# A new order for all engines, six dummy blocks, and a split of the last half step in an attention kernel

## The chip, the cores and the metric

The kernel runs on one core of a Trainium2 chip. The metric is the device time of one launch in microseconds. A profiled execution gives, beside it, the span from the first to the last recorded instruction of the core. The engines are TensorE (PE in the profile, with its weight loads as PEld), VectorE (DVE), ScalarE (ACT), GpSimd (POOL) and SyncE (SP); DMAs are issued by SyncE and, at the very start, by ScalarE.

## The reference

Two layers of attention follow each other, in 32-bit floats. Cut to what matters:

```python
# layer 1: q, k, v are (8, 8, 576, 64); row i sees keys i-63 .. i
scores = where((rel >= 0) & (rel < 64), q @ k^T / 8, -1e9)
attn = exp(scores - max); attn /= sum + 1e-9
x = (attn @ v), heads side by side            # (8, 576, 512)
# layer 2: 4 experts, each row takes the 2 with the largest logits
logits = x @ w_gate; w = softmax over the 2 chosen logits (sum + 1e-9)
for each expert e:
    a = causal softmax of (x wq[e]) (x wk[e])^T / 8      # 576 x 576
    out += (w of e where chosen) * (a @ (x wv[e]) @ wo[e])
```

## The kernel before, in words

**Stage 1 (layer 1).** The 64 heads are taken as 32 pairs, two heads side by side on the 128 partitions; a pair has nine blocks of 64 queries. Eight such blocks make a unit, and there are 36 units u. For each unit `s1_qk` computes the scores of a query block against its own and the previous key block (block letter `s`, two PSUM banks), then the softmax: copies on ScalarE, masked copies with `own`, maximum and sum on VectorE, the subtraction and the division on GpSimd (tile `sm`, small tile `st`), the exponential on ScalarE. `s1_t` transposes the weights on TensorE (`t`, tile `t`, then `ft` and `pt`) and masks them, on VectorE and GpSimd for the first nine units (`u < JOIN`, a product with `tri`), on GpSimd alone for the others. `s1_av` multiplies with v (`a`, tile `o`) and splits the result x into a high and a low part (`xh` on ScalarE, `xl` on VectorE), so that three fast products give one of full precision (`three`).

**Stage 2 (layer 2).** It goes in half steps (b, pr): batch b = 0 to 7, experts 2pr and 2pr+1. `K`, `k`, `Q`, `q` are the projections in two halves each (`kps`, `qps`, tiles `kt`, `qt`), `V` and `W` the values of a block of rows of all experts, and with them the logits, from which `s2_gate` makes the gate `g` in small steps, most on VectorE and two products on GpSimd (lines 680 and 681 of the kernel before). `1`, `2`, `3`, `4` and `0` are the scores in a burst. `s2_soft` finds row minima on VectorE (custom instruction, tile `p`) and takes the exponential on ScalarE. `s2_w` makes the factors r and multiplies p with r and g on GpSimd, nine products in a half step. VectorE transposes 32 by 32 pieces into `st`, and 16 DMAs from SyncE put these in place as `pt`; only in the last half step (`TAIL = 1`) TensorE transposes (`T`, `U`). `A` and `B` multiply with the values, `s2_o` multiplies with wo (`O`, for the last batch `o` and `O`), copies the tile and stores it.

**What sets the order.** No engine call is issued where it is written. The class `Plan` (lines 83 to 347) records all calls, links them by the tiles they use and writes each engine's queue by a simulation with costs of its own (`length`, `SWITCH`, `HOP`, `OVERLAP`). TensorE's queue is fixed by the string `ORDER`, one letter for one block, and within a letter in the order of the calls. The other engines take, among the calls that are ready in that simulation, the one with the earliest due time: what TensorE needs first, shifted by a number of its own from the table `EARLY`. All blocks of TensorE share eight PSUM banks. All instructions are therefore issued from one line, L345, and the profile is read by tiles.

## Time and profile before

| | |
|---|---|
| median of 3 runs | 425.3 us (424.87 to 425.34) |
| profiled execution, device time | 425.67 us |
| its span | 423.9 us |
| mean granted clock of TensorE | 0.984 |
| TensorE busy | 400.3 us (94%) in 5109 products |
| VectorE busy | 320.6 us (76%) |
| ScalarE busy | 266.9 us (63%) |
| GpSimd busy | 269.1 us (63%) |

The device time is the span and 1.8 us around it. Busy time counts from the start of an instruction to its end; a product of two 32-bit tiles of stage 1 shows as two records, since it takes two passes. The granted clock is the share of full speed that the chip allowed TensorE: 1.00 is 2.4 GHz, 0.50 is 1.2 GHz. In a timeline, a row with `x16` is a run of sixteen like instructions, and the bracket says how long the engine had been idle before the first of them and which engine or DMA ended that.

### The profile page before, as it was taken

To read this page: it belongs to the slowest core of one execution; us is meant where nothing else is said; L and a number is where in the kernel's file an instruction comes from. 1 tells how busy PE (TensorE), PEld (TensorE's weight loads), DVE (VectorE), ACT (ScalarE), POOL (GpSimd) and SP (SyncE) were. 2 spreads that over 40 slices of the span, in tenths; PEclk is the share of its full clock that TensorE was granted. 3 is DMA by queue.
4 is the path that set the end of the run, shared out by engine and by line. 5 is a ranking of instruction groups with operands and counts; after the bars stand their busy time and mean duration, and the time that the engine had idled before them with its cause. 6 is when DMAs were issued, how large, how long until landed. Compare 5 with 4: busy or idle time off the path is not lost.

```text
span 423.9 us, 13636 instructions
## 1 busy us (share of the span) xinstructions
PE 400.3 (94%) x5109; PEld 360.6 (85%) x5109; DVE 320.6 (76%) x1033; ACT 266.9 (63%) x845; POOL 269.1 (63%) x437
## 2 busy tenths in 40 slices
PE   4589999999999999999999999999999999998795
PEld 3478989898989989889989998988988989897584
DVE  4789998979895877779796897769788668568322
ACT  2547667676868575676668477585668755563742
POOL 4668776787697747595787749864797551505040
PEclk9669999999999999999999999999999999999999
DMA  7966672267796860676866566666775524552703
GB/s 241 331 242 207 199 234 94 65 172 236 194 318 185 251 193 3 160 199 191 278 225 161 176 167 239 169 172 173 200 202 164 123 57 114 141 140 57 184 26 125
DMA packets 34129, 74.27 MB, mean 175 GB/s; under 512 B 6416, under 2 KB 10512, under 8 KB 34064
## 3 DMA queue, kind: packets, MB, share of 16 engines
q1 hardware_dynamic: 33488, 72.88, 58.5%
q8 instruction: 41, 0.67, 0.6%
q10 hardware_dynamic: 576, 0.52, 0.4%
q14 instruction: 24, 0.20, 0.2%
HBM read 39.85 MB, written 9.44 MB: 116 GB/s over the span
## 4 chain that ended last, share of the span: by engine, by line
PE 65%; DVE 15%; SPq 5%; POOL 5%; ACT 3%; DMA 3%; issue 3%; ACTq 0%; DVEq 0%; POOLq 0%
PE o L345 14%; PE s L345 12%; PE kps L345 9%; PE qps L345 9%; PE ops L345 9%; PE v2ps L345 9%; DVE st L345 6%; SPq L345 5%; PE t L345 4%; POOL p L345 3%; DMA k<-in_kT_dram 2%; DVE p L345 2%; DVE pt L345 1%; ACT p L345 1%; DVE sm L345 1%
## 5 line engine op out<-in xcount | busy, mean ns | idle before, releaser
L345 POOL TENSOR_SCALAR p<-p,r,g 128x320 f32<-128x320 f32 (+4 forms) x144 | 88.9, 634 | 42.9 <-DVE r L345 31.4
L345 POOL TENSOR_SCALAR_AFFINE_SELECT pt<-ft 64x512 f32<-64x512 f32 x126 | 84.4, 670 | 28.1 <-ACT ft L345 20.3
L345 POOL TENSOR_TENSOR sm<-sm,st 128x512 f32<-128x512 f32 x72 | 76.0, 1057 | 37.6 <-DVE st L345 26.8
L345 ACT ACTIVATE p<-p,r 128x320 f32<-128x320 f32 (+4 forms) x144 | 83.0, 578 | 17.3 <-DVE r L345 16.8
L345 PE MATMUL o<-pt,v 128*64 128x64 f32 (+2 forms) x1820 | 84.8, 252 | 6.6 <-DMA pt<-st 2.7
L345 PEld LDWEIGHTS o<-pt,v 128*64 128x64 f32 x1820 | 73.2, 140 | 19.2 <-issue 5.7
L345 DVE STREAM_TRANSPOSE st<-p 128x64 f32<-128x64 f32 (+2 forms) x135 | 68.4, 523 | 15.3 <-POOL p L345 10.2
L345 DVE CUSTOM_DVE_ANT_0 p<-s,causal 128x320 f32<-128x320 f32 (+2 forms) x128 | 56.2, 485 | 8.5 <-PE s L345 8.2
L345 DVE TENSOR_REDUCE st<-sm 128x8 f32<-128x512 f32 x72 | 48.3, 675 | 5.5 <-ACT sm L345 4.7
L345 PE MATMUL s<-kt,qt 64*128 64x256 f32 (+2 forms) x480 | 43.5, 319 | 2.2 <-ACT qt L345 0.9
L345 PE MATMUL s<-k,q 64*64 64x128 f32 (+1 forms) x1116 | 38.5, 278 | 6.7 <-DMA k<-in_kT_dram 6.7
L345 PEld LDWEIGHTS s<-kt,qt 64*128 64x128 f32 x480 | 35.9, 185 | 8.2 <-DVE qt L345 1.4
L345 PEld LDWEIGHTS s<-k,q 64*64 64x64 f32 x1116 | 31.9, 139 | 11.1 <-DMA q<-in_qT_dram 4.4
L345 PE MATMUL qps<-xh,wqhi 128*128 128x256 f32 (+1 forms) x128 | 39.0, 304 | 0.0
L345 PE MATMUL kps<-xh,wkhi 128*128 128x256 f32 (+1 forms) x128 | 38.8, 303 | 0.1
L345 PE MATMUL qps<-xh,wqlo 128*128 128x256 f32 (+1 forms) x128 | 37.6, 294 | 0.0
L345 PE MATMUL kps<-xh,wklo 128*128 128x256 f32 (+1 forms) x128 | 37.6, 294 | 0.0
L345 PE MATMUL qps<-xl,wqhi 128*128 128x256 f32 (+1 forms) x128 | 37.6, 294 | 0.0
L345 PE MATMUL kps<-xl,wkhi 128*128 128x256 f32 (+1 forms) x128 | 37.6, 294 | 0.0
L345 PE MATMUL v2ps<-wvhi,xh 128*128 128x260 f32 x128 | 37.2, 290 | 0.0
L345 DVE COPY_PREDICATED sm<-own,s 128x256 f32<-128x256 uint8 x72 | 29.0, 436 | 10.1 <-ACT sm L345 9.4
L345 PE MATMUL v2ps<-wvhi,xl 128*128 128x260 f32 x128 | 36.3, 283 | 0.0
(109 smaller groups left out, 893.9 us busy)
## 6 DMA issues: line engine op xcount, KB each, us to landing
v<-in_vW_dram SPq DMA_DIRECT2D x28, 576.0 KB, 4.8
pt<-st SPq DMA_DIRECT2D x120, 116.0 KB, 2.3
pt<-st SPq DMA_DIRECT2D x120, 80.0 KB, 2.1
out_dram<-out SPq DMA_DIRECT2D x32, 256.0 KB, 2.3
q<-in_qT_dram SPq DMA_DIRECT2D x28, 288.0 KB, 4.5
k<-in_kT_dram SPq DMA_DIRECT2D x28, 288.0 KB, 4.5
out_dram<-out SPq DMA_DIRECT2D x8, 128.0 KB, 2.4
v<-in_vW_dram SPq DMA_DIRECT2D x3, 320.0 KB, 7.0
```

The costliest lines, as they stand in the source:

```text
L345: call(*args, **kw)
```

## The change

1. `ORDER` and `EARLY` are new throughout, and so are the costs in `Plan` (changes of shape on TensorE, 100 ns after a GpSimd operation where 40 stood, lengths of GpSimd's operations, DMAs). Every engine's queue has another order. With few exceptions, named below, the instructions are the same ones.
2. Six dummy blocks `z` are added near the start of TensorE's queue: each multiplies the identity matrix with itself twice into a PSUM bank that nobody reads.
3. In the last half step (7, 1) the factors and products are taken in four smaller parts before the last one, as scores come, and the five products with even x run on VectorE, the four others on GpSimd as before.
4. The last output tile (batch 7, j = 4) is computed in two banks of 256 columns. One is copied by VectorE, the other by ScalarE, and the second of its two stores is issued by ScalarE.
5. `own` has a second half, made by one more cast on VectorE. The function `s1_d` and the sizes with `SHORT` are not used (`TPE` is 99, `SHORT` is 0). The gate's two products on GpSimd are the same as before.

```diff
@@ order and constants
 ORDER = (
-    "ssststaatsQQtassKVtVaatssqVtkastaKt1saa2V34Wts0kVqKtVQas1324tqVV0kstKQaAaBsat132"
...
-    "VBAk132V0VVK4kABOq3Q1OO240BATOToTTUoUoUoUoUABOOOOO"
+    "szsszztzstzatzsatQssaatVKQKtassatkqVtass12tVVs3taaq4s0WtKVQqkVs1aV3240tkKVktssaA"
...
+    "0VOKVOVBAQVqk12304KABOOQkq12340OOBATToTTUoUoUoUoUABOOOOO"
 EARLY = {
-    0: -22550, 2: -1250, 3: -50, 4: 2550, 5: -7250, 6: -1450, 7: -1850, 8: 22350, 9: 51250, 10: 3450,
+    0: -900, 1: 18550, 2: -6300, 3: -2950, 4: 700, 5: 34950, 6: 3750, 7: 7200, 8: 57850, 9: 27550,
...
+SHORT = 0
+WARM = 6
+TPE = 99
@@ class Plan
-    SWITCH = {(64, 64, F32): 90, (128, 64, F32): 140, (128, 128, F32): 155, (64, 128, F32R): 180, (128, 128, F32R): 200}
-    HOP = 40
+    SWITCH = {(64, 64, F32): 130, (128, 64, F32): 170, (128, 128, F32): 130, (64, 128, F32R): 220, (128, 128, F32R): 240}
+    HOP = {e: 100 if e == "G" else 40 for e in "PVAGS"}
...
+        op["lap"] = -50 if engine == "G" and outs[0].shape[0] <= 64 else self.OVERLAP[engine]
...
-            return {"tensor_tensor": 60 + 1.97 * n, "affine_select": 190 + 0.94 * n,
-                    "memset": 100 + 0.7 * n}.get(name, (265 if outs[0].shape[0] > 64 else 190) + 0.83 * n)
+            if name == "tensor_scalar" and len(ins) > 1:
+                return 342 + 0.85 * n
+            return {"tensor_tensor": 190 + 1.67 * n, "tensor_mul": 190 + 1.67 * n, "affine_select": 170 + 0.96 * n,
+                    "memset": 100 + 0.7 * n}.get(name, 190 + 0.84 * n)
@@ dummies
+    def warm(k):
+        ps = psum.tile([128, 512], F32, tag="s", bufs=8, name=f"warm_{k}")
+        with nc.block("z"):
+            for i in range(2):
+                nc.tensor.matmul(ps[:, 0:128], lhsT=ident, rhs=ident, start=True, stop=True)
...
+    todo += [(-9.0, warm, (k,)) for k in range(WARM)]
@@ s2_soft and s2_w
         if k == 1:
             least(banks[0][:, 448:512], P2[0][:, 0:64], m_f[:, 1], r2[:, 0, 0:1])
             exp(P2[0][:, 0:64], 0)
-            s2_w(b, pr, 0)
+            if not last:
+                s2_w(b, pr, 0)
...
+        if last and k < 2:
+            for x0 in ((1, 3), (0, 5))[k]:
+                s2_w(b, pr, 0, (x0, x0 + 2 if x0 else 1))
...
-            nc.gpsimd.tensor_scalar(p, p, r2[:, 2, x:x + 1], G2[b % 2][:, pr, x:x + 1], op0=OP.mult, op1=OP.mult)
+            engine = nc.vector if last and x % 2 == 0 else nc.gpsimd
+            engine.tensor_scalar(p, p, r2[:, 2, x:x + 1], G2[b % 2][:, pr, x:x + 1], op0=OP.mult, op1=OP.mult)
@@ s2_o
+        end = b == NB - 1 and j == 4
+        banks = [psum.tile([128, DM // (1 + end)], F32, tag="s", bufs=8, name=f"ops_{b}_{j}_{i}") for i in range(1 + end)]
...
-        if b < NB - 1 or j % 2:
+        if end:
+            nc.vector.tensor_copy(t[:, 0:256], banks[0])
+            nc.scalar.activation(t[:, 256:512], banks[1], AF.Copy)
+        elif b < NB - 1 or j % 2:
...
-                nc.sync.dma_start(out[b - 1 + i, 512:576], t[64 * i:64 * i + 64])
+                (nc.scalar if i and end else nc.sync).dma_start(out[b - 1 + i, 512:576], t[64 * i:64 * i + 64])
```

Three places in the queues, as the two kernels issue them.

ScalarE's queue at its very start, before. `k_74` holds the keys of the first pair, `k_76` of the second, `k_78` of the third, `st_69` of the fourth; `sm_0` and `sm_1` are the scores of units 0 and 1.

```order
L345 DMA k_78<-in_kT_dram 128x256
L345 DMA k_74<-in_kT_dram 128x256
L345 DMA k_76<-in_kT_dram 128x256
L345 DMA st_69<-in_kT_dram 128x256
L345 ACT_TABLE_LOAD
L345 ACTIVATE sm_0_102<-s_0_1_101 128x256
L345 ACTIVATE sm_0_102<-s_0_0_100 128x64 x2
L345 ACTIVATE sm_1_109<-s_1_1_108 128x256
L345 ACTIVATE sm_1_109<-s_1_0_107 128x64 x2
```

The same after; there `k_76` holds the keys of the first pair, `k_78` of the second, `k_80` of the third, `st_71` of the fourth.

```order
L358 DMA k_78<-in_kT_dram 128x256
L358 DMA st_71<-in_kT_dram 128x256
L358 DMA k_76<-in_kT_dram 128x256
L358 DMA k_80<-in_kT_dram 128x256
L358 ACT_TABLE_LOAD
L358 ACTIVATE sm_0_110<-s_0_0_108 128x64 x2
L358 ACTIVATE sm_0_110<-s_0_1_109 128x256
L358 ACTIVATE sm_1_117<-s_1_0_115 128x64
L358 ACTIVATE sm_1_117<-s_1_1_116 128x256
L358 ACTIVATE sm_1_117<-s_1_0_115 128x64
```

The first pair's keys were the second load of the four and are the third now.

VectorE's queue around the masks of unit 4 (`pt_4`), before; `qt` and `kt` are the split of the query and key tiles of stage 2, `xl` that of x.

```order
L345 COPY_PREDICATED sm_6_168<-own,s_6_1_167 128x256
L345 COPY_PREDICATED sm_6_168<-own,s_6_0_166 128x256
L345 TENSOR_TENSOR qt_89<-qps_1_0_249,qt_89 128x192
L345 TENSOR_REDUCE st_6_169<-sm_6_168 128x8
L345 TENSOR_TENSOR xl_113<-o_2_135,xh_112 128x320
L345 TENSOR_TENSOR kt_0_211<-kps_0_0_209,kt_0_211 128x256
L345 TENSOR_REDUCE st_5_153<-sm_5_152 128x8
L345 TENSOR_TENSOR pt_4_148<-t_4_147,tri 64x4x128
L345 RECIPROCAL st_5_153<-st_5_153 128x8
L345 TENSOR_TENSOR xl_113<-o_2_135,xh_112 128x192
L345 TENSOR_TENSOR pt_4_148<-t_4_147,tri 64x4x128
```

The same after.

```order
L358 TENSOR_REDUCE st_6_177<-sm_6_176 128x8
L358 TENSOR_TENSOR pt_4_156<-t_4_155,tri 64x4x128
L358 TENSOR_TENSOR xl_121<-o_2_143,xh_120 128x192
L358 TENSOR_REDUCE st_5_161<-sm_5_160 128x8
L358 TENSOR_TENSOR pt_4_156<-t_4_155,tri 64x4x128
L358 RECIPROCAL st_5_161<-st_5_161 128x8
L358 TENSOR_TENSOR xl_121<-o_3_152,xh_120 128x320
L358 TENSOR_TENSOR kt_0_219<-kps_0_0_217,kt_0_219 128x256
L358 TENSOR_REDUCE st_6_177<-sm_6_176 128x8
L358 TENSOR_TENSOR xl_121<-o_3_152,xh_120 128x64
L358 TENSOR_TENSOR qt_91<-qps_1_0_257,qt_91 128x192
```

The subtractions for `qt_89` and `kt_0` stood ahead of the masks; as `qt_91` and `kt_0` they stand behind them now.

VectorE's queue around the gate of batch 7, before; `p_1` and `r_7_0` are rows of the softmax of the half step (7, 0), `g_7_0`, `gs`, `gt` and `g_1` the steps of the gate.

```order
L345 RECIPROCAL r_7_0_901<-r_7_0_901 128x7
L345 TENSOR_TENSOR g_7_0_884<-logits_87 128x64
L345 TENSOR_REDUCE gs_0_886<-logits_87 128x4
L345 TENSOR_TENSOR g_7_0_884<-logits_87 128x64
L345 TENSOR_REDUCE gt_0_885<-g_7_0_884 128x16
L345 TENSOR_TENSOR gt_0_885<-logits_87,gs_0_886 128x16
L345 SCALAR_TENSOR_TENSOR gt_0_885<-gt_0_885 128x16
L345 TENSOR_REDUCE gs_0_886<-gt_0_885 128x4
L345 TENSOR_SCALAR gs_0_886<-gs_0_886 128x4
L345 RECIPROCAL gs_0_886<-gs_0_886 128x4
L345 ISA p_1_68,r_7_0_901<-s_7_0_3_0_899,causal,m_7_0_902 128x256
```

The same after.

```order
L358 SCALAR_TENSOR_TENSOR gt_0_893<-gt_0_893 128x16
L358 TENSOR_REDUCE gs_0_894<-gt_0_893 128x4
L358 TENSOR_SCALAR gs_0_894<-gs_0_894 128x4
L358 RECIPROCAL gs_0_894<-gs_0_894 128x4
L358 TENSOR_TENSOR g_1_99<-gt_0_893,gs_0_894 64x4x2x2
L358 TENSOR_TENSOR g_1_99<-gt_0_893,gs_0_894 64x3x2x2
L358 TENSOR_TENSOR g_1_99<-gt_0_893,gs_0_894 64x2 x2
L358 TENSOR_TENSOR kt_0_889<-kps_0_1_891,kt_0_889 128x256
L358 ISA p_0_69,r_7_0_909<-s_7_0_0_0_901,causal 128x320
L358 ISA r_7_0_909 128x1
L358 ISA p_0_69,r_7_0_909<-s_7_0_0_1_902,causal 128x320
```

The last steps of the gate stood behind nearly all row minima of the half step, and stand ahead of the first of them now.

## Rows read from the trace of the kernel before

**Rows 1.** Busy times by stretch: length, each engine's busy us (instructions), TensorE's granted clock, DMA.
```profile
4.40:28.05 23.65, 15.71 (x237) 12.54 (x237) 17.14 (x31) 11.10 (x26) 14.34 (x21) 0.72 0.96 336
28.05:380.00 351.95, 349.35 (x4583) 319.85 (x4582) 282.87 (x929) 235.61 (x765) 239.98 (x379) 1.00 0.60 174
380.00:401.60 21.60, 17.49 (x142) 13.99 (x140) 13.53 (x53) 10.89 (x34) 5.86 (x10) 1.00 0.44 111
401.60:419.40 17.80, 17.75 (x153) 14.20 (x153) 5.64 (x15) 8.00 (x20) 5.53 (x9) 1.00 0.17 64
419.40:423.90 4.50, 0.00 (x0) 0.00 (x0) 0.68 (x1) 0.00 (x0) 0.00 (x0) 1.00 0.58 181
sum 423.90, PE 400.31 PEld 360.61 DVE 320.65 ACT 266.88 POOL 269.07; mean PE 66.72 PEld 60.10 DVE 53.44 ACT 44.48 POOL 44.84
```

**Rows 2.** TensorE's waits: what it waited for, us in total, times, longest.
```profile
PE s L345 <- DMA k<-in_kT_dram: 6.7, 4, 4.4
```

**Rows 3.** Timeline, 0 to 30 us: start, us busy, engine, line, operation, times.
```profile
4.40 1.13 PE L345 MATMUL s<-k,q 64*64 64x64 f32 x16 [4.40 <-DMA k<-in_kT_dram]
...
6.14 1.56 PE L345 MATMUL s<-k,q 64*64 64x64 f32 x28 [0.61 <-DMA k<-in_kT_dram]
...
13.49 0.66 PE L345 MATMUL t<-ident,sm 128*128 128x128 f32 x4 [2.80 <-POOL sm L345]
...
18.09 1.98 PE L345 MATMUL o<-pt,v 128*64 128x64 f32 x32
```

**Rows 4.** Busy times by stretch around the slow clock.
```profile
14.79:28.45 13.66, 10.05 (x130) 8.29 (x131) 10.60 (x16) 7.45 (x15) 10.32 (x12) 0.50 0.96 367
8.00:14.79 6.79, 3.08 (x58) 2.03 (x50) 5.55 (x13) 3.32 (x10) 3.75 (x4) 1.00 0.94 273
28.45:60.00 31.55, 30.96 (x540) 28.50 (x541) 30.19 (x62) 20.46 (x64) 22.34 (x33) 1.00 0.56 180
```

**Rows 5.** Busy times of the stretch 20 to 70 us.
```profile
20.00:70.00 50.00, 46.57 (x728) 42.12 (x727) 46.93 (x115) 33.51 (x100) 35.90 (x53) 0.92 0.64 217
```

**Rows 6.** Timeline, 180 to 188 us: unit 21's weights and its transposes.
```profile
181.45 1.04 POOL L345 TENSOR_TENSOR sm<-sm,st 128x512 f32<-128x512 f32 x1
...
186.50 0.60 PE L345 MATMUL t<-ident,sm 128*128 128x128 f32 x4
```

**Rows 7.** Timeline, 79 to 81 us: one block of scores of stage 1.
```profile
79.18 1.09 PE L345 MATMUL s<-k,q 64*64 64x128 f32 x32
79.56 0.41 DVE L345 TENSOR_TENSOR qt<-qps,qt 128x256 fp32r<-128x256 f32 x1
...
80.20 1.07 PE L345 MATMUL s<-kt,qt 64*128 64x256 f32 x12
```

**Rows 8.** Timeline, 173 to 176 us: two such blocks in a row.
```profile
173.92 1.88 PE L345 MATMUL s<-k,q 64*64 64x128 f32 x64
...
175.73 0.56 PE L345 MATMUL s<-kt,qt 64*128 64x320 f32 x4
```

**Rows 9.** Timeline, 355 to 402 us: the half steps (6,1) and (7,0).
```profile
355.26 2.47 PE L345 MATMUL s<-kt,qt 64*128 64x256 f32 x30
...
361.80 5.53 POOL L345 TENSOR_SCALAR p<-p,r,g 128x64 f32<-128x64 f32 x9 [7.66 <-DVE r L345]
...
372.03 2.11 PE L345 MATMUL s<-kt,qt 64*128 64x256 f32 x24
...
383.08 5.54 POOL L345 TENSOR_SCALAR p<-p,r,g 128x64 f32<-128x64 f32 x9 [2.69 <-DVE g L345]
...
389.96 10.03 SPq L345 DMA_DIRECT2D pt<-st  x16
...
401.60 2.96 PE L345 MATMUL o<-pt,v 128*64 128x256 f32 x44 [2.39 <-DMA pt<-st]
```

**Rows 10.** Timeline, 417 to 424 us: the last copy and the stores.
```profile
417.31 3.94 SPq L345 DMA_DIRECT2D out_dram<-out  x6
...
419.38 0.69 DVE L345 COPY out<-ops 128x512 f32<-128x512 f32 x1 [0.71 <-PE ops L345]
```

More of the change, by code (lines that the diff above doesn't have):

```diff
@@ L125, in length @@
         if name == "dma_start":
-            return (475 if min(x.shape[0] for x in outs + ins if x.space == bass.MemoryType.SB) == 128 else 635)
+            return (450 if min(x.shape[0] for x in outs + ins if x.space == bass.MemoryType.SB) == 128 else 635)
         psum = any(x.space == PSUM for x in ins)
@@ L162, in link @@
             for x, w in op["use"]:
-                if x.space not in (PSUM, bass.MemoryType.SB):
+                if x.space == DRAM and not hasattr(x.tensor, "tag"):
                     continue
                 t = x.tensor.name
-                box = self.box(x)
+                box = (0, 1, 0, 1) if x.space == DRAM else self.box(x)
                 bank = x.space == PSUM
@@ L287, in order @@
                     o["wait"] -= 1
-                    o["ready"] = max(o["ready"], now + (0 if o["engine"] == op["engine"] else self.HOP))
+                    o["ready"] = max(o["ready"], now + (0 if o["engine"] == op["engine"] else self.HOP[o["engine"]]))
                     if not o["wait"]:
@@ L327, in order @@
                 best["start"] = now
-                clock[e] = best["pend"] = now + max(20, cost - self.OVERLAP[e])
+                clock[e] = best["pend"] = now + max(20, cost - best["lap"])
                 end = now + cost + (200 if e == "P" else 0)
@@ L439, in window_attention_moe_attention @@
     load_weight(3)
-    own = const.tile([128, 64], mybir.dt.uint8, name="own")
+    own = const.tile([128, 2, 64], mybir.dt.uint8, name="own")
     m_f = const.tile([128, 2, 64], F32, name="m_f")
@@ L475, in split_weights @@
         whi[name], wlo[name] = hi, lo
-    NU = NB * NP * BLK // 8
+    SIZES = [4] * SHORT + [8] * ((NB * NP * BLK - 4 * SHORT) // 8)
+    STARTS = [sum(SIZES[:u]) for u in range(len(SIZES))]
+    NU = len(SIZES)
     def later(p):
@@ L492, in tiles @@
     def tiles(u):
-        for i in range(8):
-            yield i % 2, i // 2, *ORDER[8 * u + i]
+        for i in range(SIZES[u]):
+            yield i % 2, i // 2, *ORDER[STARTS[u] + i]
     def s1_qk(u):
@@ L557, in s1_av @@
         t = PT1.pop(u)
+        size, w, start = SIZES[u], SIZES[u] // 2, STARTS[u]
         o = psum.tile([128, 8, 64], F32, tag="s", bufs=8, name=f"o1_{u}")
@@ L573, in s1_av @@
                 XL[b9] = work.tile([128, NP * S], F32R, tag="xl", name=f"xl{b9}")
-            at = [S * (p % NP) + 64 * b for p, b in ORDER[8 * u + i:8 * u + i + n]]
+            at = [S * (p % NP) + 64 * b for p, b in ORDER[start + i:start + i + n]]
             j = 0
@@ L772, in s2_soft @@
         r2, m2 = R2[b, pr], M2[b, pr]
+        last = 2 * b + pr >= 2 * NB - TAIL
         banks = SB.pop((b, pr, k))
```

113 lines of the change are left out of this document (72 added, 41 removed), and 67 rows, old and new, of the table EARLY.

## The prediction

> **What bounds the kernel now.** I read the busy time by stretch first, then TensorE's waits, then the timeline of the stretches that have idle time. The reader is to see in the busy times [rows 1] that TensorE works 400.31 of 423.90 us, and where the other 23.6 lie: 4.4 before its first product (0 to 4.40, not a row), 7.94 of the 23.65 us up to 28.05, only 2.60 of the 351.95 us up to 380.00, 4.11 up to 401.60, 0.05 up to 419.40, and 4.50 at the end, when the last tile is copied and stored. So the kernel is bound by TensorE, with a slow start, one hole late and a fixed end. A new order can gain only in those holes, or by making TensorE's own work shorter; in the 352 us of the middle it can mostly lose.
>
> The waits say who is late at the start: the largest sum is a load of keys, 6.7 us in 4 waits [rows 2]. In the timeline of the start [rows 3] TensorE waits for that load at 4.40, again at 6.14, then 2.80 us at 13.49 for the weights of the first unit from GpSimd, and its first product with v is at 18.09. The granted clock is 0.50 from 14.79 to 28.45, that is 1.2 GHz, and 1.00 (2.4 GHz) before and after; between 8.00 and 14.79 TensorE had been busy 3.08 of 6.79 us, and in the slow stretch 10.05 of 13.66 [rows 4]. From 20 to 70 us VectorE is busy 46.93 of 50.00 us [rows 5]: behind the start it is VectorE that sets the pace, not TensorE.
>
> **The change part by part.** The sum is made against the profiled execution, 425.67 us; the median of the runs, 425.3, is 0.37 lower, and that is taken off at the end.
>
> *The start: dummies, loads and order.* In the new order the keys of the first pair are third in ScalarE's queue and not second. Before, 16 of the first unit's 32 product records ran at 4.40 and the rest followed at 6.14, where the third load had landed; now all 32 come after that. By the 28 records that took 1.56 [rows 3] the 16 cost 16 x 0.056 = 0.9 us on the way to the first softmax. The six dummy blocks are four passes of 128 columns each; the nearest row is a block of four such passes, 0.60 [rows 6], so 3.6 us in all at 2.4 GHz and 7.2 at 1.2. TensorE is idle 7.94 us in this stretch, and four of the six stand where it waited: one ahead of the third pair's scores (0.61 idle at 6.14), two ahead of the first transposes (2.80 idle at 13.49), one behind them. The cover of the other two is gone if their inputs come sooner, and then they cost up to 1.2 each. What decides is VectorE, since it is full. In front of the masks of unit 4 two subtractions of the query and key tiles stood ahead and stand behind now; one takes 0.41 [rows 7], so 0.8 us. One cast is added (a few tenths at a time when VectorE has 4 us to spare). I take -0.8, since the full engine is the nearest to a limit. The bounds: +0.9, when the later first scores are passed on whole, and -2.0, when units 1 to 4 are all pulled forward (VectorE has 3.07 us to spare in its 50 us, and two thirds of that are taken).
>
> *Fewer changes of shape on TensorE.* Its queue has 117 places in the old order, and 108 in the new, where products of another shape of weights follow. One block of scores took 1.02 us from its start to that of the next block (79.18 to 80.20) [rows 7], two in a row 1.81 (173.92 to 175.73) [rows 8]; that is 0.23 less than two single ones, for two changes that are saved, so 0.115 each. Nine of them: -1.0. Bounds: by the busy times alone (1.09 and 1.88) it is 0.15 each, -1.35; if half of the nine lie where TensorE waits anyhow, -0.5.
>
> *The middle.* All else that is moved there keeps its kind and number. TensorE has 2.60 us of waits to give back, so the gain is at most 2.6; a loss has no such bound and stands among the rivals. I take 0.
>
> *The hole before 401.60.* For batch 7's first half step the scores start at 372.03, the products of GpSimd at 383.08 (they waited for the gate on VectorE), the stores of transposed weights at 389.96, and TensorE has the weights back at 401.60: 29.57 us [rows 9]. For the half step before it the same way from scores to products took 355.26 to 361.80, 6.54 us [rows 9], since no gate was late. In the new order all the value blocks and with them the gate stand ahead of these scores, so I put 6.54 in place of 11.05. The way is then 6.54 + 5.54 (nine products) + 1.34 (388.62 to 389.96) + 11.64 (389.96 to 401.60) = 25.06 us. But what TensorE does meanwhile shrinks too: 25.46 us before (29.57 less the 4.11 of idle time, all of it behind 380.00 [rows 1], of which 2.39 is the last), and by the blocks of the new order, with their old durations, 3.9 less, 21.6. The hole is then 25.06 - 21.6 = 3.5 in place of 4.1: -0.6. The gate's own instructions stay where they were, two on GpSimd among them, whatever the change is called. Bounds: the stores are sixteen issues on SyncE, 10.03 us; where two issues of output stand among them (3.94 for 6, so 1.3 for two [rows 10]) it is +0.7, and -2.0 where the stores of finished columns start before the last product does.
>
> *The last half step's products on two engines.* Five of nine products leave GpSimd for VectorE, whose 5.64 of 17.80 us busy [rows 1] has room. But TensorE is busy 17.75 of 17.80 us there: nothing waits for these products, so 0. Should TensorE reach these transposes sooner by one block of output that moved ahead, the split covers what would come out as a wait. Bounds 0 and -0.5.
>
> *The last tile.* Now one copy of 0.69 starts at 419.38 and ends at 420.07, and then SyncE issues two stores, up to 421.25 (417.31 + 3.94) [rows 10], 1.18 us behind it, 0.59 each. After: two half copies side by side, about 0.35 to 0.45, and two issues side by side on two queues: -0.3 - 0.59 = -0.9. Bounds -0.5 (ScalarE's copy and issue start later, by the step from one engine to the other) and -1.0.
>
> Sum: -0.8 - 1.0 + 0 - 0.6 + 0 - 0.9 = -3.3, so 422.4 for an execution like the profiled one, and **422.0** for the median. This term by term forecast holds within 420.7 and 423.4 if no new wait comes.
>
> **A rule on the clock.** The row shows a granted clock of 0.50 behind a stretch in which TensorE was busy 45% [rows 4]. The Trainium skill says, in "TensorE: Matmul & The Clock Gate", section "What's actually happening", that "the default state is throttled, and activity releases the throttle". By it dummies count as activity though they compute nothing, and the fast clock would last; by the rows alone, which have no dummies, the clock falls as before. The trace agrees in so far as the clock fell behind idle time; that dummies hold it no row shows. This gives the second rival below.
>
> **Rivals.**
> - *New waits in the middle.* 35 units are laid anew, and some products now stand sooner behind what they need. The clearest is the transposes of unit 21: GpSimd's last operation on its weights ended at 182.49, TensorE came at 186.50 [rows 6], 4.0 us later; in the new order 4.7 us less of TensorE's work stands ahead of them, which leaves a wait of 0.7 to 1.0. Two products with v (units 3 and 18) come out likewise at 0.9 and 0.4. Against it: GpSimd and VectorE have idle time there (239.98 and 282.87 of 351.95 [rows 1]), so their work may come sooner too. With 2.3 us lost: 424.3.
> - *The clock stays up.* 10.05 us of products at 0.50 would be 5.0 [rows 4]; VectorE can give back only its 3.07 idle us [rows 5]. With 3.1 more: 418.9. For it: four dummies stand in the very stretch in which TensorE was busy 45%. Against: the stretch 14.79 to 28.45 was 74% busy and stayed slow.
> - *Slower: the start is lost.* The first scores 0.9 later, and three dummy blocks on the path at 1.2 each, as the clock is 0.50: +4.5, against -2.5 of the other terms: 427.7, that is 427.3 for the median. It decides from a loss of 2.9 at the start, seen by the first product with v starting after 21.0 (18.09 before). For it: VectorE has no room to make up for a late start. Against: before the first transposes TensorE had 2.80 us of idle time.
> - *The change gives nothing*: the new order's waits eat what the end gives, 425.0.
>
> **How the numbers follow.** Forecast 0.46, new waits 0.20, clock 0.14, slower 0.14, nothing 0.06. This kernel's measurement can tell about 0.2% from no change, that is 0.85 us: faster is below 424.45, slower above 426.15. Faster: 0.46 + 0.14 + 0.12 (of the new waits) = 0.72. Slower: 0.14 + 0.02. The rest, 0.12, is the same. The range of 8 in 10 reaches from the clock's case, 418.7, to the upper half of the new waits, 425.2; it leaves out the slower case and the far end of the clock's.
>
> **What would show it.** Right: the last copy and stores end some 3.6 us behind the last product and not 4.5; the waits of TensorE ahead of the first products for batch 7 sum to about 3.5; the first product with v between 17 and 19 us; TensorE's busy time about 1 us lower without the dummies. Wrong: a clock of 1.00 throughout from 8 to 28 us (then the clock's case); more than 4 us of idle time between 28 and 380 (new waits); the first product with v after 21 (slower).

## The result: slower by 0.8%, not faster

| | before | after |
|---|---|---|
| median of 15 runs each, same chip | 426.84 us (424.38 to 430.74) | 430.8 us (428.23 to 436.5) |
| ratio | | 1.0079, 95% interval 1.0053 to 1.0105 |
| the changed kernel once more, 12 runs | 426.54 us | 430.1 us, ratio 1.0049 (1.0014 to 1.0084) |

The forecast was 422.0 us, 0.8% faster, with a range up to 425.2; 1.0079 times the median it set out from, 425.3, is 428.7. Both sign and range were wrong. The ratios leave out executions that are more than 1.5% above the fastest of their kernel; both profiles of the changed kernel, of 436.5 and 431.05 us, are of such executions, and the second (span 429.3) is the one shown below.

Busy times by stretch of that profile; the columns are those of [rows 1]: length, busy us (instructions) of TensorE, its weight loads, VectorE, ScalarE and GpSimd, then TensorE's granted clock, the DMA share and GB/s.

```profile
5.92:28.72 22.80, 14.98 (x260) 12.61 (x260) 17.53 (x32) 11.80 (x29) 13.97 (x16) 0.99 0.95 331
28.72:380.00 351.28, 345.34 (x4524) 316.91 (x4525) 277.20 (x902) 228.99 (x743) 240.54 (x377) 0.99 0.59 172
380.00:407.43 27.43, 24.09 (x204) 20.87 (x204) 20.51 (x85) 17.65 (x62) 8.55 (x14) 0.99 0.52 132
407.43:425.27 17.84, 17.84 (x153) 14.23 (x153) 6.23 (x15) 6.13 (x14) 1.13 (x1) 0.92 0.12 47
425.27:429.30 4.03, 0.00 (x1) 0.00 (x0) 0.11 (x1) 0.39 (x1) 0.00 (x0) 0.77 0.63 213
```

TensorE is idle 5.92 us ahead of the first product (4.40 before), 7.82 up to 28.72 (7.94), 5.94 in the middle (2.60), 3.34 ahead of 407.43 (4.11), nothing in the last stretch and 4.03 at the end (4.50). Two of the forecast's holes did shrink. What grew is the wait for the first keys, the middle, and TensorE's busy time, 402.25 us against 400.31, in which the six dummies are counted.

Its waits, largest first (what waited for what, us in total, times, longest):

```profile
PE t L358 <- POOL sm L358: 7.0, 5, 3.6
PE s L358 <- DMA k<-in_kT_dram: 5.9, 1, 5.9
PE o L358 <- DMA pt<-st: 3.8, 3, 2.6
PE o L358 <- issue: 1.4, 2, 1.2
```

The load of keys fell from 6.7 to 5.9 us [rows 2]; the weights that GpSimd makes, 7.0 us in five waits, are now the first. TensorE's timeline of the start answers to [rows 3]:

```profile
5.92 1.99 PE L358 MATMUL s<-k,q 64*64 64x64 f32 x32 [5.92 <-DMA k<-in_kT_dram]
7.83 1.22 PE L358 MATMUL warm<-ident 128*128 128x128 f32 x4
...
11.90 1.16 PE L358 MATMUL warm<-ident 128*128 128x128 f32 x8
15.47 0.66 PE L358 MATMUL t<-ident,sm 128*128 128x128 f32 x4 [2.41 <-POOL sm L358]
...
18.57 1.29 PE L358 MATMUL o<-pt,v 128*64 128x64 f32 x32
...
23.34 0.67 PE L358 MATMUL s<-k,q 64*64 64x64 f32 x16 [1.36 <-DMA q<-in_qT_dram]
...
28.72 0.69 PE L358 MATMUL t<-ident,sm 128*128 128x128 f32 x2 [3.63 <-POOL sm L358]
```

The scores start 1.52 us later; the two dummy blocks (`warm`) ahead of the first transposes stand in a wait, as foreseen, and the first product with v starts at 18.57. Yet at 28.72 TensorE waits 3.63 us more. That wait doesn't come from the dummies: kernel 10, which has none near the start and is among the fastest, has it too, at 28.14, and 7.0 us in five such waits.

```profile
28.14 0.87 PE L479 MATMUL t<-ident,sm 128*128 128x128 f32 x4 [3.48 <-POOL sm L479]
```

And the slow stretch of the clock has moved. Windows around it, this kernel first, then the same order without dummies (experiment 2), then kernel 10:

```profile
8.00:13.00 5.00, 5.00 (x76) 4.26 (x76) 3.03 (x7) 2.20 (x7) 1.04 (x1) 1.00 1.00 336
13.00:28.00 15.00, 7.90 (x153) 6.59 (x152) 13.78 (x25) 9.21 (x20) 12.21 (x14) 1.00 0.99 355
28.00:32.00 4.00, 3.28 (x20) 3.15 (x20) 3.37 (x5) 1.12 (x2) 2.91 (x4) 0.57 0.04 12
```

```profile
12.00:23.00 11.00, 8.12 (x92) 6.28 (x92) 9.17 (x19) 7.66 (x16) 9.00 (x10) 0.53 1.00 352
23.00:28.00 5.00, 2.35 (x53) 2.07 (x54) 4.97 (x10) 1.86 (x6) 4.20 (x5) 1.00 1.02 371
28.00:32.00 4.00, 4.00 (x103) 3.78 (x103) 3.88 (x8) 3.27 (x11) 3.02 (x5) 1.00 0.24 74
```

```profile
12.00:23.00 11.00, 6.26 (x97) 4.79 (x101) 9.42 (x18) 7.77 (x16) 9.50 (x10) 0.84 1.04 363
28.00:32.00 4.00, 3.86 (x28) 3.64 (x32) 2.82 (x5) 1.50 (x5) 2.73 (x5) 0.57 0.02 6
```

Before, 1.2 GHz was granted from 14.79 to 28.45 [rows 4]. With the dummies the clock is 2.4 GHz there, and falls behind the wait that ends at 28.72, where TensorE has work: the twelve products for `qps` take from 29.49 to 31.96 there, and from 27.81 to 29.39 in kernel 2. But this isn't the mark of the dummies either. Kernel 10 has the fall behind 28 us without them, kernel 16, which is the same kernel, was at 1.2 GHz from 15.94 to 26.18 and not behind 28, and kernel 15, without early dummies, was at 2.4 GHz up to 29.73.

### The profile page after: what moved, and what is told of

It is laid out like the page before. It is cut to its first block, busy times and chain, and to the rows that moved or that the text cites. A ratio compares the mean times of both kernels' runs of the same rounds, so it can differ in the third digit from the quotient of the medians.

```text
span 434.8 us, 13688 instructions
## 1 busy us (share of the span) xinstructions
PE 404.1 (93%) x5139; PEld 367.1 (84%) x5139; DVE 323.9 (74%) x1042; ACT 266.5 (61%) x849; POOL 268.2 (62%) x432
## 4 chain that ended last, share of the span: by engine, by line
PE 76%; DVE 9%; SPq 3%; ACT 3%; POOL 3%; DMA 2%; issue 2%; ACTq 0%; DVEq 0%; POOLq 0%
PE o L358 16%; PE s L358 13%; PE qps L358 11%; PE v2ps L358 11%; PE kps L358 10%; PE ops L358 10%; PE t L358 4%; SPq L358 3%; DVE st L358 3%; POOL sm L358 2%; DMA pt<-st 1%; DVE sm L358 1%; DVE pt L358 1%; DVE p L358 1%; ACT p L358 1%
## 5 line engine op out<-in xcount | busy, mean ns | idle before, releaser
L358 POOL TENSOR_SCALAR p<-p,r,g 128x448 f32<-128x448 f32 (+4 forms) x139 | 87.1, 643 | 45.1 <-DVE r L358 29.8
L358 PE MATMUL o<-pt,v 128*64 128x64 f32 (+2 forms) x1820 | 87.1, 254 | 9.2 <-DVE p L358 3.5
L358 PEld LDWEIGHTS o<-pt,v 128*64 128x64 f32 x1820 | 75.2, 141 | 22.1 <-issue 4.6
L358 PE MATMUL s<-k,q 64*64 64x128 f32 (+1 forms) x1116 | 37.3, 280 | 7.2 <-DMA k<-in_kT_dram 6.2
L358 PE MATMUL qps<-xh,wqhi 128*128 128x320 f32 (+1 forms) x128 | 39.3, 307 | 0.0
L358 PE MATMUL qps<-xl,wqhi 128*128 128x320 f32 (+1 forms) x128 | 38.2, 298 | 0.0
L358 PE MATMUL qps<-xh,wqlo 128*128 128x320 f32 (+1 forms) x128 | 38.2, 298 | 0.0
L358 PE MATMUL v2ps<-wvlo,xh 128*128 128x260 f32 x128 | 36.1, 282 | 0.0
```

The costliest lines, as they stand in the source:

```text
L358: call(*args, **kw)
```

## The experiments

Three theories were to be told apart. One: the dummies cost, by TensorE's time on them or by the clock phase that they move. Two: the new order costs, by waits in its start or its middle, and the dummies do no harm. Three, formed when one and two fell: dummies cost by merely standing early in the queue.

Kernels 2 to 16 and 18 issue every engine's queue from a list, word for word, so that the planner can't move anything. Unless a diff says otherwise, the other four engines' queues are those of the changed kernel. In the diffs stands the head (and where it matters the tail) of TensorE's queue, one letter for one block, `z` a dummy. Ratios are to the kernel before on the same chip, with 95% intervals, of 12 runs each (7 in experiment 7, 6 in 14, 17 and 18).

**1. The change once more**

```diff
  "szsszztzstzatzsatQssaatVKQKtass...OOBATToTTUoUoUoUoUABOOOOO"
```


> The changed kernel once more, to have a profile of a fast execution and its ratio beside the variants on the same chip. Every theory expects about 1.008 times the kernel before, some 428.7 us. Theory S (the start is lost: later first scores and dummies) expects most of the 3.4 us as idle time of TensorE before 30 us; theory M (new waits in the middle) expects at least 2.5 us more idle time between 60 and 380 us than the 2.6 before; theory T (the tail) expects a longer hole ahead of batch 7's last products with the values.

1.0049 (1.0014 to 1.0084): the loss is there again, somewhat smaller.

**2. No dummies**

```diff
- "szsszztzstzatzsatQssaat...
+ "ssststatsatQssaat...
```


> The changed kernel's order of every engine, word for word, without the six dummy blocks. If the dummies cost what they took in the way of the first units (theory S, dummies), it is 1.5 to 3 us faster than the changed kernel, some 426 to 427 us. If they hold the clock and so pay, it is 1 to 4 us slower, 430 to 433. By theory M it is the same as the changed kernel within 0.5 us.

0.9983 (0.9947 to 1.0020). The loss goes with the dummies alone.

**3. The start of before, no dummies**

```diff
- "szsszztzstzatzsatQssaatVKQK...
+ "ssststaatsQQtassKVtVaatssqV...   (all queues: before's order for 58 us, then the new one)
```


> The order before for all that was issued in about the first 58 us, the changed order for everything behind it, no dummies. Theory S expects the start's loss to be gone: 425 to 426 us or better (the end's 0.9 stays gained). Theory M expects 428 to 429, the waits of the middle being still there.

1.0007 (0.9980 to 1.0034): behind the old start the new middle gives nothing that can be measured.

**4. The kernel before with six dummies**

```diff
- "ssststaatsQQtass...   (all queues: before)
+ "szsszztzstzaatzsQQtass...
```


> The kernel before with the six dummy blocks at the same places of TensorE's queue as in the changed kernel, nothing else. If the dummies stand in idle time, no difference within 0.5 us; if they delay the first units, 1.5 to 3 us slower, some 427 to 428; if they keep the granted clock at 1.00 from 14.8 to 28.4 us, up to 3 us faster.

1.0058 (1.0029 to 1.0088). Six dummies cost the old order as much as the new one. So it isn't something in the new order that makes them dear.

**5. The new start without dummies in front of the old middle**

```diff
- "ssststaatsQQtassKVtV...   (all queues: before, with the new last half step and last tile)
+ "ssststatsatQssaatVKQKtass...
```


> The changed order without dummies for what was issued in about the first 58 us, the order before for everything behind it, and the changed last half step and last tile. The changed kernel without dummies was 2.1 us ahead of the kernel before from 25 to 60 us and lost it again later. If the new waits of the middle took it back (theory M), this keeps the 2.1 of the start and some 0.7 of the end: 422 to 423.5 us, ratio 0.993 to 0.996. If any middle takes it back, since the waits come from units that VectorE and GpSimd are late with, it is 425 within 0.7.

1.0073 (1.0047 to 1.0100), with no dummy in it. A start that does no harm in one kernel costs 0.7% in front of another middle; so a loss of this size can come without them. Why it does here stays open.

**6. The kernel before with the new last half step and last tile**

```diff
- engine = nc.gpsimd
+ engine = nc.vector if last and x % 2 == 0 else nc.gpsimd     (and the two half copies)
```


> The order before up to the last half step, then the changed last half step (products on two engines) and last tile (two half copies, two queues for the stores). By my term for the end: 0.9 us faster, 0.5 to 1.0, and nothing from the products. The rival: the second store's issue on ScalarE and the landing come no earlier, no difference within 0.3 us.

1.0005 (0.9972 to 1.0039): the end's 0.5 us isn't resolved.

**7. Five more dummies in the wait ahead of 28.72**

```diff
- "szsszztzstzatzsatQ...
+ "szsszztzstzatzsazzzzztQ...
```


> The changed kernel with five more dummy blocks in TensorE's idle time from 25.1 to 28.7 us, ahead of the transposes of unit 3. If the loss of the dummies comes from the slow clock, which they only put off from 12 to 22 us to 28 to 32 us, where TensorE waits for nothing, these keep it at 1.00 there and the time is 1 to 1.5 us below that of the changed kernel. If it comes from the softmax of the first units, which the dummies delay, no difference within 0.5 us, and the granted clock changes all the same.

1.0097 (1.0061 to 1.0133). Five dummies in a wait gain nothing; whether they cost more isn't resolved against the 1.0079 (1.0053 to 1.0105) and 1.0049 of the changed kernel.

**8. Without the first dummy**

```diff
- "szsszztzstzatzsatQ...
+ "ssszztzstzatzsatQ...
```


> The changed kernel without the first of its six dummy blocks, the one ahead of the third pair's scores, which took 1.15 us on the way of unit 1. If the delay of the first softmax is the cause (VectorE takes its queue in order, so that unit 0's sums wait behind unit 1's masked copies), it is 1.2 to 1.4 us faster than the changed kernel. If the late slow clock is, no difference within 0.5 us.

0.9999 (0.9959 to 1.0040). The twelve times spread from 421.8 to 432.3 us, and their median, 428.19, is 0.45% above that of the kernel before, 426.28. So this run doesn't decide what the first dummy costs.

**9 to 11. Four dummies in the wait at 25 us, in the hole near 399 us, in both**

```diff
- "ssststatsatQ...OOBATToTTU...
+ "ssststatsazzzztQ...OOBATToTTU...          (9)
+ "ssststatsatQ...OOzzzzBATToTTU...          (10)
+ "ssststatsazzzztQ...OOzzzzBATToTTU...      (11)
```


> The changed order without its six dummy blocks, and four dummy blocks only where TensorE waits from about 25.3 to 27.4 us, ahead of the transposes of unit 3. No unit is delayed by them. If dummies cost by the delay of the first units (theory D), the time is that of the changed kernel without dummies, 425.7 within 1, and the start's order on VectorE runs within 0.3 us of it. If every dummy block costs its own time, it is 2 us slower than that. The granted clock behind 28 us should be 1.00.

> The changed order without its six dummy blocks, and four dummy blocks only in the hole of about 2.7 us ahead of the products with the values of the half step (7,0), near 399 us. In five of seven traces with that hole the granted clock fell to 0.5 for some 3.4 us behind it, which costs 1.7. If dummies hold the clock, 1 to 1.7 us faster than without, 424 to 425; if not, no difference.

> Both sets of four dummy blocks, in the hole at 25 us and in the one at 399 us, and none of the six. By the clock theory the fastest of all, 423.5 to 425; if dummies pay nothing, 425.7 within 1.

1.0046 (1.0009 to 1.0082), **0.9968 (0.9938 to 0.9997)**, 1.0054 (1.0020 to 1.0088). At the end of the queue the same four dummies cost nothing, and in kernel 10 the clock stays up: in the stretch behind the hole, without and with them,

```profile
400.00:408.00 8.00, 6.81 (x61) 5.63 (x62) 2.96 (x9) 2.88 (x9) 1.85 (x2) 0.79 0.23 80
```

```profile
399.00:408.00 9.00, 8.15 (x84) 7.08 (x82) 5.46 (x20) 5.56 (x19) 3.21 (x4) 1.00 0.38 111
```

(2, then 10). In kernel 11 the granted clock is 1.00 nearly throughout, also at the start:

```profile
8.00:28.00 20.00, 13.78 (x218) 11.23 (x213) 16.60 (x31) 11.55 (x29) 12.86 (x15) 1.00 0.99 351
28.00:60.00 32.00, 30.75 (x514) 28.93 (x514) 30.50 (x69) 21.00 (x65) 24.90 (x34) 1.00 0.57 189
```

and it is slower than kernel 10 all the same. Nor do its early dummies hold up what follows: the wait that they stand in still lasts 1.54 us behind them. So neither a slow clock nor TensorE's time on the dummies is the cause of the loss. That late dummies hold the clock isn't certain: it fell behind this hole in 10 of the 14 traces without late dummies, and in one (kernel 18) of the six with them.

**12. The new end and four late dummies on the kernel before**

```diff
- "ssststaatsQQ...240BOATToTTU...   (all queues: before, new last half step and last tile)
+ "ssststaatsQQ...240zzzzBOATToTTU...
```


> The order before with the changed last half step and last tile, and four dummy blocks in its hole near 397 us. Against the same without dummies (427.4 median): 0 to 1.7 us faster by the clock theory, more than 0.5 us slower if dummies cost their own time.

1.0000 (0.9972 to 1.0027), against 1.0005 without them (6): no difference. In neither trace does the clock fall behind that hole, so there was nothing to hold up.

**13 and 14. Dummies ahead of the first scores; dummies behind the wait at 25 us**

```diff
- "ssststatsatQssaat...
+ "zzzssststatsatQssaat...       (13)
+ "ssststatsatzzzzQssaat...      (14)
```


> The changed order without its six dummy blocks, and three dummy blocks ahead of TensorE's first scores, while it waits for the first keys until 5.9 us. They delay nothing and stand far from the slow phase of the clock. If dummies cost only by what they delay or by the clock, the time is that without dummies, 425.7 within 1; if any dummy costs, whatever it stands in, 1.3 to 2 us slower.

> As e9 (four dummy blocks, none of the six), but the four stand behind the transposes of unit 3 and not in the wait ahead of them, where TensorE has work without end: they cost their own 2.2 us, so 2 to 3 us slower than without dummies. If the ones in the wait cost the same (e9: 2.7 us), the wait did not hide them.

1.0082 (1.0043 to 1.0120) and 1.0100 (1.0051 to 1.0150, 6 runs). Three dummies at a time when TensorE has nothing at all to do cost 1.0% against kernel 2.

**15 and 16. Kernel 10 with the keys loaded in the order of the pairs; kernel 10 again**

```diff
- DMA k_78, st_71, k_76, k_80   (ScalarE's first four; kernel 10 and 16)
+ DMA k_76, k_78, k_80, st_71   (15)
```


> The kernel of e10 (changed order, no dummies near the start, four in the hole at 399 us) with the keys of the pairs loaded in the order 1, 2, 3, 4, so that the first scores start near 4.4 us and not 5.9. By my term for the loads 0.9 us faster than e16; if the first units wait for VectorE and GpSimd anyhow, the same within 0.5.

> The kernel of e10 on the same chip as e15, the control for it: 0.997 of the kernel before, some 425.

0.9970 (0.9938 to 1.0003) and 0.9962 (0.9931 to 0.9993). In 15 the first scores start at 4.25 instead of 6.3 us, and nothing of that is left in the time. Kernel 10 is faster than both kernels in either measurement.

**17 and 18. Dummies of 4 columns**

```diff
- nc.tensor.matmul(ps[:, 0:128], lhsT=ident, rhs=ident, start=True, stop=True)
+ nc.tensor.matmul(ps[:, 0:4], lhsT=ident, rhs=ident[:, 0:4], start=True, stop=True)
```

(17: all six of the changed kernel; 18: the early four of kernel 11.)

> The changed kernel, every engine's instructions in the same order, but each of the twelve products of the six dummy blocks computes 4 columns and not 128 (the results of the dummies are read by nobody). TensorE's queue has the same number of instructions in the same places. Theory 1, the dummies' work is what costs (time on TensorE, and the slow stretch of the clock moved to 28 to 32 us): nearly all of the loss goes, and it comes to the kernel without dummies, ratio 0.996 to 1.000, with the granted clock 0.50 from some 13 to 24 us again. Theory 2, the mere presence of more instructions early in TensorE's queue costs, by what it shifts in all that comes later: ratio stays at 1.004 to 1.008, and the waits near 100 and 344 us stay.

> The kernel with four dummies in TensorE's wait at 25 us and four in its hole at 399 us (1.0054), with the four early ones cut from 128 to 4 columns per product; the late four stay as they are. Theory 1 (work of the early dummies): ratio 0.995 to 0.999, as the kernel with the late four alone (0.9968 and 0.9962). Theory 2 (presence of the instructions): 1.003 to 1.008, with the wait of some 2.6 us near 344 us still there.

1.0201 (1.0153 to 1.0249) and 1.0115 (1.0054 to 1.0176). Kernel 17 tells nothing: its queues are still written by the planner, which takes shorter dummies into account, and the other engines' order came out otherwise between some 12 and 40 us, against what the expectation says (TensorE waits 7.91 us at 34.31). Kernel 18 has every queue of kernel 11, but its edit took less away than was meant. The sixteen records of the early dummies in 18, then in 11:

```profile
24.78 1.95 PE L479 MATMUL warm<-ident 128*128 128x4 f32 x16
```

```profile
25.44 2.05 PE L479 MATMUL warm<-ident 128*128 128x128 f32 x16
```

With 4 columns TensorE is busy 1.95 us on them, with 128 columns 2.05. So 18 says that fewer columns don't help, and not that dummies without any time of their own cost as much. That it isn't their time is read from where TensorE falls behind, in the next section.

## Where the loss sits: a fetch that meets a transfer

All kernels with the changed order run the same 5115 products besides the dummies, in one order. So each product's start can be set beside that of the same product in kernel 10. By how many us TensorE is later than kernel 10, in one profile of each, at these times of kernel 10:

| kernel | early dummies | 95 us | 110 us | 200 us | 340 us | 345 us | end |
|---|---|---|---|---|---|---|---|
| 16 | 0 | -1.9 | -1.9 | -2.7 | -1.0 | -1.0 | -1.3 |
| 2 | 0 | -2.2 | -2.9 | -3.8 | -2.2 | -1.3 | 0.1 |
| 9 | 4 | -1.5 | -1.5 | -3.5 | -0.6 | 4.0 | 4.4 |
| 11 | 4 | -0.6 | -0.6 | -1.0 | 2.1 | 4.9 | 4.6 |
| 13 | 3 | 1.0 | 3.5 | 2.4 | 4.1 | 6.3 | 6.6 |
| 18 | 4 | 0.3 | 2.9 | 2.4 | 5.0 | 7.9 | 9.4 |
| 1 | 6 | 0.3 | 4.4 | 2.8 | 5.8 | 6.0 | 6.1 |

At 95 us none of these kernels is behind kernel 10 by more than 1.0 (kernel 14, whose dummies stand in no wait, by 2.0). So most of the loss isn't at the dummies. It comes in a few places long behind them, and which ones differs from kernel to kernel.

TensorE has 5131 products and 5131 weight loads in kernel 10. Among its DMA queues (packets, MB, share of 16 engines) is this one:

```profile
q8 instruction: 41, 0.67, 0.7%
```

41 packets of 16 KB, one for about 250 TensorE instructions, some 10 us apart: by their number these are the fetches of TensorE's code (a second queue of this kind, q14, moves smaller packets and isn't counted here). An early dummy block puts eight more records (four products, four loads) ahead of all that follows, and so moves every later fetch against the other engines' work. Two DMAs of transposed weights (`pt<-st`) show what that does, each the last of its batch. First SyncE and VectorE near 322 us, kernel 10, then kernel 9 (start, us busy, engine, operation, times, idle time before and who ended it):

```profile
314.46 8.13 SPq L479 DMA_DIRECT2D pt<-st  x13
```

```profile
323.97 0.92 DVE L479 STREAM_TRANSPOSE st<-p 128x64 f32<-128x64 f32 x3 [1.68 <-DMA pt<-st]
```

```profile
313.75 8.14 SPq L479 DMA_DIRECT2D pt<-st  x13
```

```profile
325.05 0.87 DVE L479 STREAM_TRANSPOSE st<-p 128x64 f32<-128x64 f32 x3 [3.63 <-DMA pt<-st]
```

VectorE, which may not overwrite `st` before the DMA has read it, goes on 1.38 us behind the last issue (322.59) in kernel 10, and 3.16 behind it (321.89) in kernel 9. The DMA traffic between, by queue and kind (packets, MB, share of 16 engines), 322.6 to 324.1 in kernel 10 and 321.8 to 325.0 in kernel 9:

```profile
q1 hardware_dynamic: 168, 0.34, 81.7%
```

```profile
q1 hardware_dynamic: 225, 0.44, 46.6%
q8 instruction: 1, 0.02, 3.2%
```

In kernel 9 one fetch falls into it. Twenty us later TensorE waits for the next batch of these transfers (kernel 9, then 18):

```profile
345.04 1.55 PE L479 MATMUL o<-pt,v 128*64 128x256 f32 x6 [2.82 <-DMA pt<-st]
```

```profile
350.55 1.71 PE L479 MATMUL o<-pt,v 128*64 128x256 f32 x17 [2.72 <-DMA pt<-st]
```

That wait isn't only the delay passed on from 322 us: the last transfer of this next batch meets a fetch of its own. In kernel 9 it is issued up to 341.97 (first fence), a fetch starts as the issue ends, and it lands 2.98 us behind it, at 344.95; in kernel 10 (second fence) no fetch starts for 1.9 us, it lands in 1.50, and TensorE has no wait.

```profile
331.90 10.07 SPq L479 DMA_DIRECT2D pt<-st  x14
```

```profile
331.44 9.39 SPq L479 DMA_DIRECT2D pt<-st  x14
```

In kernel 9 the clock falls too, to 0.50 from 344.90 to 348.31, and the 44 products behind the wait take 4.55 us and not the 2.96 of other batches.

Another place is near 96 us. In the changed kernel the last `pt<-st` is issued at 96.22, a fetch starts 0.77 later, the weights land at 99.41, and TensorE, which has been idle, goes on at 99.60 (first fence; its bracket names no releaser); in kernel 2 the fetch starts 1.70 later, and TensorE has no wait (second fence, its row of the same products, no bracket).

```profile
97.25 1.15 PE L358 MATMUL o<-pt,v 128*64 128x64 f32 x32
99.60 1.59 PE L358 MATMUL o<-pt,v 128*64 128x256 f32 x33 [1.21 <-issue]
```

```profile
94.72 4.50 PE L479 MATMUL o<-pt,v 128*64 128x64 f32 x100
```

Read the same way out of the packets and landings of each kernel with this order (start of the fetch and landing, both in us behind the issue's end; the landing here is that of the whole DMA):

| kernel | early dummies | 96 us: fetch, landing | 322 us: fetch, landing | 342 us: fetch, landing | late of 15 | ratio |
|---|---|---|---|---|---|---|
| 16 | 0 | 1.09, 1.46 | 3.04, 1.47 | 2.41, 1.51 | 2 | 0.9962 |
| 10 | 0 | 2.39, 1.47 | 3.32, 1.48 | 1.92, 1.50 | 1 | 0.9968 |
| 15 | 0 | 1.39, 1.47 | 3.56, 1.48 | 1.67, 1.51 | 1 | 0.9970 |
| 2 | 0 | 1.70, 1.46 | 3.51, 1.50 | 1.10, 1.51 | 2 | 0.9983 |
| 8 | 5 | 1.19, 1.48 | -1.96, 1.48 | 1.27, **3.34** | 2 | 0.9999 |
| 9 | 4 | 1.07, 1.46 | 0.00, **3.06** | 0.00, **2.98** | 4 | 1.0046 |
| 1 | 6 | 0.77, **3.19** | -2.81, 1.47 | 1.09, 1.51 | 4 | 1.0049 |
| 11 | 4 | 1.09, 1.47 | 0.26, **3.19** | 0.18, **3.12** | 4 | 1.0054 |
| 7 | 11 | 0.06, **2.62** | none near, 1.48 | -2.49, 1.51 | 2 | 1.0097 |
| 13 | 3 | 0.59, **3.22** | -0.03, **3.04** | 0.00, **2.30** | 4 | 1.0082 |
| 14 | 4 | 0.72, **3.20** | 0.77, **2.81** | 1.49, **3.56** | 5 | 1.0100 |
| 18 | 4 | 0.73, **3.14** | 0.59, **2.94** | 0.68, **3.05** | 4 | 1.0115 |

Each kernel has fifteen such batches, and the column "late of 15" counts the last transfers that land more than 2.2 us behind their issue. In these twelve profiles and the first one of the changed kernel that is 195 last transfers: 155 land in 1.46 to 2.00 us and 40 in 2.30 to 3.71. Where a fetch starts from -0.03 to 0.78 us behind the issue's end, all 35 are late. The five other late ones have a fetch 0.80 to 1.49 behind, where sixteen more with a fetch between 1.07 and 1.49 are in time, so that the edge isn't sharp. And all 40 land 1.07 to 1.51 us behind the end of the fetch's own packet. Within a batch it is less clear: of all 3120 `pt<-st` transfers of these traces, 181 came more than 1 us above the median of the same transfer, and a fetch started from -0.3 to 0.75 us around the issue's end in 110 of these and in 176 of the other 2939.

The count goes with the early dummies (1 or 2 without, 2 to 5 with), but it doesn't give the time: kernel 7 has two late ones at 1.0097, kernel 8 two at 0.9999, and kernel 5 (order of before behind 58 us, no dummies) none at 1.0073. In kernel 4, whose other queues are before's, two of fifteen are late, at 114.6 and 284.4 us, and none is in the kernel before. Set beside that kernel product by product, it is 0.8 us behind up to 110 us, 2.0 at 120 and 2.7 at 300; most of the rest of its 4.4 comes behind 400 us, where the clock is at 0.50 from 404.03 to 407.44.

The Trainium skill says in "Runtime: NRT & Kernel Launch", section "Instruction fetch mechanics", that an engine's instructions are brought in by its own DMA queue in blocks of 16 KiB, 256 instructions, and that the cost of crossing to the next block is "mostly hidden". The trace agrees with the size (41 packets for 10,262 records). What TensorE itself pays at a crossing no run here shows; a late last transfer stands at a block: 1.46 to 2.00 us in time, 2.30 to 3.71 late.

What is shown is that early dummies cost the time (1 against 2, 4 against the kernel before, 11 and 18 against 10), that the loss comes long behind them, and that late landings come with it and a fetch stands at each. That the fetch causes the late landing rests on these counts; no run here moved a fetch alone. The two waits of TensorE behind late landings in kernel 18 are 1.24 and 2.72 us, 4.0 of the 6.3 us that it is slower than kernel 10 (1.0115 less 0.9968, of 426 us), so not all of it.

Two rivals. Any shift of the start may cost as much by chance, whatever it is made of: against that stands kernel 15, whose first scores start 2 us sooner than those of kernel 10, and whose time is the same; for it stands kernel 5. And a dummy takes one of the eight PSUM banks, which could make later blocks wait for another bank. In the programs of kernels 9 and 2 the block that held a bank before is another one for 6 of 450 blocks, all right behind the dummies (units 3 to 5 and what stands between); 109 blocks sit in a bank of another number, and what that does no run separates.

## Why the prediction was wrong, point by point

Two steps failed: the price of the dummies in the start's term, and the middle, which was put at nothing. With the dummies taken out (kernel 2) the ratio is 0.9983, 424.6 us on the forecast's base of 425.3. So of the 6.7 us between the forecast of 422.0 and the 428.7 measured, some 4.1 go with the dummies (2.8 by the second measurement) and 2.6 with the order itself.

- **Start, -0.8: the first step that failed.** A dummy was priced by TensorE's time on it, nothing where it waited and up to 1.2 where not. Dummies in pure waits (9, 11, 13, and with fewer columns 18) cost 0.6 to 1.5% against the same order without them, and the cost comes behind 95 us, where the sum had no term for them. The rest of the step agrees in size, but loosely: without dummies the new start saved 0.2 to 2.4 us, and kernels 10 and 16, which are one kernel, stand at 0.2 and 2.1. That is from what TensorE's blocks are late by against the sum of the old durations of all blocks ahead, at some 85 us: before 24.7 us, kernels 2, 10, 15 and 16 22.3, 24.5, 24.5 and 22.6, the changed kernel 24.9.
- **Switches of shape, -1.0.** Not measured apart. Kernel 2 keeps TensorE busy 397.1 us against 400.3, but of these 3.2 some belong to the shorter slow stretch (8.12 us of work in it, 10.05 before).
- **Middle, 0: the second step that failed.** The sign named for new waits, over 4 us idle between 28 and 380, came: 5.94. It came without dummies too, 5.72 us in kernel 2 and 4.0 to 5.3 in kernels 10, 15 and 16, against 2.60 before:

```profile
27.40:380.00 352.60, 346.88 (x4581) 319.04 (x4582) 281.23 (x930) 232.34 (x755) 241.49 (x379) 1.00 0.60 175
```

  So 1.4 to 3.1 us stand against a term of nothing. They aren't where the rival put them; no wait of unit 21 (186 us) is in the trace, and in the changed kernel 1.21 of them stand behind the late landing at 96 us. What causes the others stays open.
- **Hole, -0.6: right, in its steps too.** 3.34 us idle ahead of the first products for batch 7 against the 3.5 that were worked out (4.11 before). The scores of the half step start at 382.71, and from there:

```profile
388.88 5.55 POOL L358 TENSOR_SCALAR p<-p,r,g 128x64 f32<-128x64 f32 x9 [7.41 <-DVE r L358]
395.79 10.03 SPq L358 DMA_DIRECT2D pt<-st  x16
407.43 2.83 PE L358 MATMUL o<-pt,v 128*64 128x256 f32 x12 [2.62 <-DMA pt<-st]
```

  That is 24.72 us for the 25.06 of the sum, and TensorE's work in it 21.4 for 21.6. But the last wait is still 2.62 us, and the clock falls behind it, which it didn't do before (1.00 [rows 1]): 0.92 over the 17.84 us behind the hole, 1.4 us. That took the gain back. In kernel 10, with late dummies, the clock stayed up there, and kernel 2 loses 1.6 us against it from 400 to 405 us; the ratios, 0.9968 and 0.9983, don't resolve it.
- **Last half step, 0: right.** TensorE is busy 17.84 of 17.84 us there.
- **Last tile, -0.9: mis-sized, -0.6.** The span ends 4.03 us behind the last product against 4.60 (that product ended at 419.35; the stretch in [rows 1] begins at 419.40). The last copies and issue, of the changed kernel:

```profile
424.61 1.09 ACT L358 ACTIVATE out<-ops 128x512 f32<-128x512 f32 x2 [0.80 <-PE ops L358]
...
424.96 0.43 DVE L358 COPY out<-ops 128x256 f32<-128x256 f32 x1 [0.36 <-PE ops L358]
...
425.73 0.55 ACTq L358 DMA_DIRECT2D out_dram<-out  x1
```

  The last issue ends at 426.28, 1.01 behind the last product (425.27), where it was 1.90 (421.25 less 419.35 [rows 10]): 0.89 sooner, as worked out. But from there to the end of the span it is 3.02 us against 2.70. The way of the store itself, which the sum took as fixed, grew by 0.3. It is so in other traces: 3.02 to 3.04 with the new end (kernels 1, 2, 5, 6, 10, 12, 16), 2.70 with the old one (before and 4). Which of store, queue or engine does it no run separates.
- **The clock rival** had its sign, 2.4 GHz from 8 to 28 us, and not its gain. TensorE waited there for GpSimd and VectorE, and the slow stretch went to 28 to 32 us. In kernel 11 even that is gone, for nothing. The sign was a poor one: kernel 15 shows it without early dummies. The Trainium skill has the rule that the prediction cites, in "TensorE: Matmul & The Clock Gate", section "What's actually happening": activity releases the throttle. Kernels 10 and 11 agree, where dummies stand in a wait: the clock is 1.00 behind it, from 399 to 408 us in kernel 10 (0.79 in kernel 2), and from 28 us on in kernel 11 (0.57 up to 32 in kernel 10). Kernel 18 doesn't: with the same four late dummies it fell at 411.20.
- **The slower rival** had the sign by another way. Its sign, the first product with v after 21.0, did not come (18.57), and its price of 1.2 a block is not what was paid: at 95 us TensorE is 0.3 us behind kernel 10 and 2.2 behind kernel 16. That the outcome lies near its 427.3 is chance.

## What to carry to other kernels

An instruction that was put where an engine waits wasn't free here: it moves that engine's later instruction fetches against the other engines' DMAs, and where a fetch began with the last transfer of a batch, that one landed in 2.3 to 3.7 us and not in 1.5. So before an order is called better or worse by some tenths of a per cent, look where the packets of kind "instruction" fall against the transfers that someone waits for, and try the same edit at the end of the queue, where nothing comes behind it. A clock that is held up can pay only in a stretch where the engine has work to do: at the start of kernel 11 it paid nothing. And look at one kernel's profile more than once: 10 and 16 are one kernel, and stand 1.9 us apart at 95 us.
